# Eight small weight loads in front of the second to fourth K block instead of one per block: a grouped-query attention step on one core

## The chip, the cores and the metric

One NeuronCore of a Trainium2 chip. The metric is the device time of one execution in microseconds (us). A trace's span is 1.8 us shorter than the time of its own execution, so a span must not be compared with a time. A run is called slow when it is over 1.5% above the fastest run of the same kernel in its rounds, and fast otherwise; ratios use fast runs alone.

## The reference

Eight sequences of four query tokens, 32 query heads, 8 key/value heads of 128, a cache of 2048 positions, all bf16.

```python
q = (x @ wq).reshape(B, Sq, Hq, Dh).transpose(0, 2, 1, 3)
k, v = jnp.repeat(k_cache, rep, axis=1), jnp.repeat(v_cache, rep, axis=1)
p = softmax(einsum("bhqd,bhkd->bhqk", q, k) * Dh ** -0.5)
o = einsum("bhqk,bhkd->bhqd", p, v)
out = o.transpose(0, 2, 1, 3).reshape(B, Sq, Hq * Dh) @ wo
```

The caches are 67 MB and have to be read once: 32 blocks of K and 32 of V, 1 MB each (two heads of one sequence, 128 partitions of 8 KB). wq and wo are 4 MB each.

## The kernel before

All loads go out on one queue (the Sync engine's) in one list. The part of wo that is multiplied early is cut so that 480 of its rows lie on 40 partitions; they come in eight small loads of 5 partitions x 12 rows x 1 KB, 60 KB each.

```python
    def load_wo_e(i):
        hi, m = divmod(i, 4)
        rows = wo[: NE * WE, :].rearrange("(q r) j -> q r j", r=WE)      # NE = 40, WE = 12
        a, b = hi * 32 + m, hi * NE // 2 + m
        nc.sync.dma_start(wo_e[a : a + 17 : 4, :, :], rows[b : b + 17 : 4, :, :])
    ...
    load_k(0)
    nc.sync.dma_start(wq_sb[:, :, :], wq.rearrange("(p r) n -> p r n", r=R))
    nc.sync.dma_start(x_sb[:, :], x.flatten_outer_dims())
    loads = []
    for u in range(NU + KA):
        if 1 <= u <= 8:
            loads.append(("e", u - 1))           # one small load in front of each of eight K blocks
        if 0 < u < NU:
            loads.append(("k", u))
        ...
        if u >= KA - 1 and u - KA + 1 < NU:
            loads.append(("v", u - KA + 1))
    ...
    nc.gpsimd.memset(wo_e[:, :, :], 0.0)         # the first small load waits for this, to 5.97 us
```

One thing is not in the code: the framework has eight semaphores for DMAs and hands them out in turn, so each issue waits until the load eight places ahead of it has landed. The Sync queue issues in order, and one that waits holds up all behind it.

The softmax here doesn't subtract the row's maximum and nothing guards it: scores larger than these inputs give would overflow.

## Time and profile before

| | before |
|---|---|
| timed runs, us | 189.18, 189.28, 189.49 |
| the execution that was profiled, us | **192.02** (span 190.2) |
| chain that ended last | 97% DMA |
| DMA, 16 to 51 us / 51 to 170 us | 389 / 424 GB/s |
| TensorE busy | 83% |

How to read it: the chain that ended last is followed back from the last instruction to whatever each step waited for, and 97% of it are loads. So the kernel is one long stream of reads from HBM, and everything else keeps up with it.

### The profile page before, as it was taken

How to read it: one execution, taken by the hardware profiler on the slowest of the kernel's cores; microseconds unless marked ns; L12 is line 12 of the kernel's file. 1: busy time of each engine (PE TensorE's matmuls, PEld its weight loads, DVE VectorE, ACT ScalarE, POOL GpSimd, SP SyncE). 2: the span in 40 equal slices, each digit the busy share in tenths (PEclk: the TensorE clock that was granted, in tenths of full speed). 3: DMA queues.
4: the chain of work that ended last, by engine and by line, in shares of the span. 5: the costliest groups of instructions: out<-in, count | busy, mean ns of one | idle time of the engine just before them, and what ended most of it. 6: DMA issues, size and time to landing. Idle time of an engine off the chain costs nothing.

```text
span 190.2 us, 6461 instructions
## 1 busy us (share of the span) xinstructions
PE 156.9 (83%) x2899; PEld 139.3 (73%) x2899; DVE 113.0 (59%) x218; ACT 86.4 (45%) x170; POOL 6.3 (3%) x9
## 2 busy tenths in 40 slices
PE   0536596999978888999988999978888889999693
PEld 0516396899967777889977888878877778886471
DVE  0580545577756666757766666665666668676420
ACT  2003656565555555445555555554555554454000
POOL 8400000000000000000000000000000000000000
PEclk9999879999999999999999999999999999999858
DMA  6999999999999999999999999999999999999970
GB/s 245 451 407 382 383 394 394 386 385 387 397 419 426 422 426 424 426 422 427 424 424 426 426 422 431 417 427 422 426 424 427 420 429 420 424 424 415 416 310 22
DMA packets 10955, 75.97 MB, mean 399 GB/s; under 512 B 1288, under 2 KB 1416, under 8 KB 2568
## 3 DMA queue, kind: packets, MB, share of 16 engines
q1 hardware_dynamic: 10880, 75.55, 96.4%
q8 instruction: 22, 0.36, 0.7%
q14 instruction: 5, 0.04, 0.1%
q10 hardware_dynamic: 48, 0.02, 0.0%
HBM read 75.53 MB, written 0.03 MB: 397 GB/s over the span
## 4 chain that ended last, share of the span: by engine, by line
DMA 97%; SPq 1%; issue 0%; PE 0%; ACT 0%
DMA k_sb<-in_k_cache_dram 69%; DMA v_sb<-in_v_cache_dram 8%; DMA wo_e<-in_wo_dram 8%; DMA wq_sb<-in_wq_dram 7%; DMA wo_sb<-in_wo_dram 4%; SPq L131 0%; PE out_ps L376 0%; SPq L111 0%; ACT out_sb L430 0%; SPq L121 0%
## 5 line engine op out<-in xcount | busy, mean ns | idle before, releaser
L195 PE MATMUL kp<-ident,k_sb 128*128 128x128 f32 x512 | 82.7, 288 | 20.5 <-DMA k_sb<-in_k_cache_dram 10.5
L202 DVE COPY kt<-kp 128x1024 bf16<-128x1024 bf16 x96 | 65.5, 686 | 28.3 <-PE kp L195 27.4
L266 ACT ACTIVATE probs<-s_ps 64x256 bf16<-64x256 f32 x128 | 48.5, 379 | 69.9 <-PE s_ps L256 69.1
L195 PEld LDWEIGHTS kp<-ident,k_sb 128*128 128x128 f32 x512 | 55.8, 144 | 23.9 <-DMA k_sb<-in_k_cache_dram 12.5
L256 PE MATMUL s_ps<-q_bd,kt 128*128 128x64 bf16 x1024 | 42.5, 195 | 3.1 <-ACT kt L200 1.9
L256 PEld LDWEIGHTS <-kt 128*128 128x128 bf16 x1024 | 40.0, 99 | 5.5 <-ACT kt L200 2.2
L280 PEld LDWEIGHTS <-v_sb 128*128 128x128 bf16 x1024 | 34.4, 96 | 9.5 <-DMA v_sb<-in_v_cache_dram 2.1
L200 ACT COPY kt<-kp 128x1024 bf16<-128x1024 bf16 x32 | 32.4, 1012 | 12.6 <-PE kp L195 11.8
L280 PE MATMUL o_ps<-probs,v_sb 128*128 128x32 bf16 x1024 | 35.1, 177 | 1.2 <-DMA v_sb<-in_v_cache_dram 1.1
L302 DVE TENSOR_REDUCE l_sb<-l_ps 128x32 f32<-128x512 f32 x32 | 22.1, 692 | 21.2 <-PE l_ps L294 21.2
L294 PE MATMUL l_ps<-probs,ones 128*128 128x512 bf16 x64 | 19.0, 379 | 0.0
L306 DVE RECIPROCAL r_sb<-l_sb 128x32 f32<-128x32 f32 x32 | 11.3, 353 | 1.1
L311 DVE TENSOR_TENSOR oT<-o_ps,r_sb 128x32 bf16<-128x32 f32 x32 | 5.8, 182 | 1.9 <-PE o_ps L280 1.7
L294 PEld LDWEIGHTS <-ones 128*128 128x128 bf16 x64 | 6.1, 98 | 0.5
L430 ACT CAST out_sb<-out_ps 64x256 bf16<-64x256 f32 x1 | 0.4, 366 | 13.1 <-PE out_ps L376 13.1
L376 PE MATMUL out_ps<-wo_sb,oP 128*32 128x256 bf16 x48 | 5.5, 393 | 0.1
L171 POOL MEMSET wo_e<- 64x6144 bf16 x1 | 5.2, 5212 | 0.3 <-POOLq L447 0.3
L243 DVE CAST q_bd<-pse 64x512 bf16<-64x512 f32 x4 | 2.6, 683 | 4.3 <-PE pse L234 4.3
L376 PEld LDWEIGHTS <-oP 128*32 128x32 bf16 x48 | 3.5, 137 | 1.4 <-issue 0.2
L178 DVE COPY pick<-ident 128x64 bf16<-128x64 bf16 x4 | 0.6, 220 | 6.5 <-POOL ident masks.py:199 6.5
L219 PE MATMUL psq<-xT_sb,wq_sb 128*128 128x32 bf16 x128 | 3.5, 186 | 0.3 <-DVE xT_sb L213 0.3
L219 PEld LDWEIGHTS <-wq_sb 128*128 128x128 bf16 x128 | 3.5, 103 | 0.3 <-issue 0.3
(41 smaller groups left out, 31.9 us busy)
## 6 DMA issues: line engine op xcount, KB each, us to landing
k_sb<-in_k_cache_dram SPq DMA_DIRECT2D x32, 1024.0 KB, 19.6
v_sb<-in_v_cache_dram SPq DMA_DIRECT2D x32, 1024.0 KB, 19.4
wq_sb<-in_wq_dram SPq DMA_DIRECT2D x1, 4096.0 KB, 14.1
wo_sb<-in_wo_dram SPq DMA_DIRECT2D x4, 512.0 KB, 14.8
wo_sb<-in_wo_dram SPq DMA_DIRECT2D x4, 256.0 KB, 9.6
wo_m<-in_wo_dram SPq DMA_DIRECT2D x1, 512.0 KB
wo_e<-in_wo_dram SPq DMA_DIRECT2D x8, 60.0 KB
x_sb<-in_x_dram SPq DMA_DIRECT2D x1, 32.0 KB
```

The source lines that it names most:

```text
L195: nc.tensor.transpose(kp[:, j, :], k4[:, w : w + 128], ident4[:, :])
L200: nc.scalar.copy(out=kt2, in_=kp2)
L202: nc.vector.tensor_copy(out=kt2, in_=kp2)
L219: nc.tensor.matmul(psq[:, h, :], lhsT=wq_sb[:, r, hh * 128 : (hh + 1) * 128], rhs=xT_sb[:, r, :], start=(r == 0), stop=(r == R - 1),)
L256: nc.tensor.matmul(s_ps[:, 2 * j : 2 * j + 2, :], lhsT=k_t[:, j % (HC // 4), :, e], rhs=q_bd[:, p, e, b, :, :], start=(e == 0), stop=(e == 1),
L266: nc.scalar.activation(out=pr[rows, hf * HC : (hf + 1) * HC, cols], in_=s_ps[rows, :, cols], func=EXP)
L280: nc.tensor.matmul(o_ps[u][:, :], lhsT=vs[u][:, cc, :], rhs=pr[:, cc, :], start=(cc == 0), stop=(cc == C - 1),)
L294: nc.tensor.matmul(l_ps[:, :, :], lhsT=ones[:, :], rhs=pr[:, c : c + LC, :], start=(c == 0), stop=(c + LC == C),)
L302: nc.vector.tensor_reduce(out=l_sb[:, :], in_=l_ps[:, :, :].rearrange("d c q -> d q c"), axis=AX, op=ADD)
L306: nc.vector.reciprocal(r_sb[:, :], l_sb[:, :])
L311: nc.vector.tensor_tensor(out=oT[(p + 1) // 2][:, :, (p == 2) * 1, b, :], in0=o_ps[u][:, :].rearrange("d (h s) -> d h s", h=HP), in1=r_sbs ...
L376: nc.tensor.matmul(out_ps[half * T : (half + 1) * T, :], lhsT=o, rhs=w[:, half * DH : (half + 1) * DH], start=(p == 0 and r == 0), stop=(p ...
```

## The change

The intent is to have the small loads out of the way early: three in front of k1, two in front of k2, three in front of k3, and from then on only blocks of 1 MB.

```diff
     for u in range(NU + KA):
-        if 1 <= u <= 8:
-            loads.append(("e", u - 1))
+        loads += [("e", i) for i in {1: (0, 1, 2), 2: (3, 4), 3: (5, 6, 7)}.get(u, ())]
         if 0 < u < NU:
             loads.append(("k", u))
```

## The prediction

> **What bounds the kernel now.** I read the page's DMA rows first, then the chain that ended last, then one table by stage, then the issues of the DMA queue in order of time, and last the single packets.
>
> ```profile
> span 190.2 us, 6461 instructions
> ...
> PE 156.9 (83%) x2899; PEld 139.3 (73%) x2899; DVE 113.0 (59%) x218; ACT 86.4 (45%) x170; POOL 6.3 (3%) x9
> ...
> DMA  6999999999999999999999999999999999999970
> GB/s 245 451 407 382 383 394 394 386 385 387 397 419 426 422 426 424 426 422 427 424 424 426 426 422 431 417 427 422 426 424 427 420 429 420 424 424 415 416 310 22
> ...
> DMA 97%; SPq 1%; issue 0%; PE 0%; ACT 0%
> DMA k_sb<-in_k_cache_dram 69%; DMA v_sb<-in_v_cache_dram 8%; DMA wo_e<-in_wo_dram 8%; DMA wq_sb<-in_wq_dram 7%; DMA wo_sb<-in_wo_dram 4%; SPq L131 0%; PE out_ps L376 0%; SPq L111 0%; ACT out_sb L430 0%; SPq L121 0%
> ```
>
> The reader should see that the chain is 97% DMA and that the DMA engines are busy from the second slice to the end, so only two things move the time: gaps in the DMA stream, or its speed. There are no gaps to take. But the GB/s row has a step: about 385 in slices 4 to 11, about 424 after. The table by stage (us, busy time of the engines, then clock, DMA share, GB/s) places it:
>
> ```profile
> 16.00:51.00 35.00, 30.83 (x595) 27.85 (x595) 19.54 (x36) 20.42 (x42) 0.00 (x0) 0.95 1.01 389
> 51.00:170.00 119.00, 106.79 (x2042) 96.96 (x2039) 79.50 (x153) 60.79 (x121) 0.00 (x0) 1.00 1.01 424
> ```
>
> The DMA share is 1.01 in both rows, so the engines weren't idle in the slow one; each packet took longer. The trace's packet records say so: a packet of 8 KB took 309 ns before 16 us, 342 ns from 16.1 to 51.1 us, and 309 ns from then on to about 170 us, all engines alike. When one engine was held for 1.1 us by an instruction fetch in the slow stretch, the packets of the others fell to 324 ns. So a shared limit holds there (16 x 8192 B / 342 ns = 383 GB/s), and each engine's own pace later. The loads that this change moves stand in exactly that stretch:
>
> ```profile
> 5.97 0.84 SPq L131 DMA_DIRECT2D wo_e<-in_wo_dram  x1
> ...
> 8.55 0.70 SPq L131 DMA_DIRECT2D wo_e<-in_wo_dram  x1
> 9.29 0.44 SPq L111 DMA_DIRECT2D k_sb<-in_k_cache_dram  x1
> 15.26 0.33 SPq L121 DMA_DIRECT2D v_sb<-in_v_cache_dram  x1
> ...
> 36.29 0.70 SPq L131 DMA_DIRECT2D wo_e<-in_wo_dram  x1
> ```
>
> The first one's packets run at 14.4 to 14.9 us, the last one's at 49.9 to 50.5 us, and its semaphore is complete at 51.16 us: within 0.3 us of the place where packets become fast again. What "wo_e loads in the queue" does to the other engines' packets I can't read from the trace; that the two stretches coincide at both ends I can.
>
> **What the Trainium skill says.** "DMA: Bandwidth & Descriptors", section "Why a DMA increments its semaphore by 16 and not by 1": a load of 5 partitions from the Sync queue is split over 5 DMA engines, the lowest-numbered ones, and the sequencer writes the other 11 counts itself. The trace agrees: the fourth such load (issued at 15.63) has a late group of five counts, at 27.50 to 27.72 us, and from k2 on each 1 MB block completes in two groups, with five counts late (k2: 20.29 to 20.85, and 21.14 to 21.38). Same page, section "Queues, rings and completion order": one engine consumes descriptors in ring order. So these rows cost time on five engines only, and an order changes which packet is early, not how much those five have to move. "HBM Reference", section "Specifications (TRN2)": a core that streams alone gets about 425 GB/s, held by its 16 DMA engines. The fast stretch shows 424; 389 is below that for no reason that the page gives.
>
> **The change, part by part.** No byte, instruction or engine changes, apart from order in the Sync queue: the order of the instructions shows SP alone altered (k1, k2 and k3 now behind 3, 5 and 8 of the small loads). There are eight semaphores for DMAs, used in turn, so an issue waits for the landing of the one eight places ahead of it.
>
> 1. The slow stretch gets shorter (the gain). I follow the five slow engines, ring order x, e0, e1, e2, k1, e3, e4, k2, e5, e6, e7, k3. They finish wq at 14.4 us. Three e packets at about 0.48 us (460 to 507 ns seen) end at 15.9; k1, eight packets at 0.34, at 18.5; e3 and e4 at 19.5; k2 at 22.2; e5 to e7 at 23.7; the last lands some 0.6 us later, at 24.3. The slow stretch would last from 16.1 to about 24 us, 8 us instead of 35. A slow us does 309/342 = 0.904 of a fast one's work, so it loses 0.096 us. Before: 35.0 x 0.096 = 3.4 us. After: 8 x 0.096 = 0.8 us. Gain 2.6 us. All of it is on the path, since the five engines are the last ones and have no gaps to absorb it.
>
> 2. New waits of the queue (no cost expected). k2 is now the tenth issue and waits for wq, complete at 15.24 us; before, it went out at 8.07. The eleven engines without small rows have k1 until 14.4 + 8 x 0.309 = 16.9 us; k2 issued at 15.26 moves some 0.8 us later (the first load: issued 0.73, first packet 1.5), at 16.1. Margin 0.8 us. k3 waits behind three issues of 0.70 us, goes out at about 17.9 and moves at 18.7, while k2 lasts to 19.3 there. v0 waits for k1 on the slow five (landed about 19.2), moves at 20.0, and k3 lasts to about 22. Thin margins, but even where one fails, only those eleven engines idle, which are ahead of the five anyway. The five always have something queued.
>
> 3. Early K blocks land later. On the slow five k1, k2 and k3 land at about 19.2, 22.9 and 27.0 us instead of 18.2, 21.4 and 25.0. TensorE is still at the projection of x then: in order of time its first transpose of k1 starts at 23.88 us, of k2 at about 28 and of k3 at about 31, so each has 4 us of slack. Its later pace, one unit per 4.12 us (norms at 40.08, 44.20, 48.32), is faster than the DMA's 2 x 2.44 = 4.9 us, so a delay would be made up. Cost 0.
>
> 4. Buffers. v6 needs v0's buffer, free at 39.15 us (first write of oT). Its semaphore comes free at about 39.3 in the new order, so the two meet, and the queue then holds seven blocks of 1 MB, 17 us of work. Cost 0.
>
> Sum: 189.28 - 2.6 = 186.7 us if the slow stretch follows the loads.
>
> **The rivals.** (a) The slow stretch belongs to time or to these blocks, not to the small loads (say the way HBM is read while the sixteen engines stand close together in one block). For it: wo_e packets move in only 4.9 of its 35 us, eleven engines never touch wo_e and slow down too, and 15 to 16 us is fast although e0 was then just done. Against it: both ends coincide with the loads. The work of the five is then the same and the time stays at 189.3. (b) The spread between the engines makes it fast: by 51 us the last engines stood over 3 us behind the first. The small loads make that spread, and the change makes it by 24 us rather than 51, so this gives nearly the same gain, about 186.7. (c) The queue starves at 16 to 20 us because k2 waits for wq, with only k1 left in flight: if the margins of part 2 are wrong by 1 us on all engines, +0.5 to +1 us. (d) The whole slow stretch goes, since k1's part of it is the only one left: -3.4 us, and the seven e packets at 460 instead of 507 ns give 0.3 more on the five: 185.6, the most that I can find.
>
> **Range and chances.** I give (step 1 or b) about 0.68, (a) 0.22, (c) without the gain 0.05, (d) 0.05. The centre moves a little from 186.7 towards 189.3: 187.0. The range 185.7 to 189.4 takes in (d) on one side and no effect on the other. Faster by 2% means under 185.5, which is beyond (d): 0.05. Slower by 2% (193.1) has no mechanism that I can see: 0.02. Within 2%: 0.93.
>
> **What would show it right or wrong.** GB/s at 24 to 51 us near 424 instead of 389, 8 KB packets at 309 ns there, and the slow stretch ending when the last wo_e load lands: step 1 right. Still 389 until 51 us: (a). If it turns fast later than 24 us but before 51, (b) is nearer. A DMA share under 0.95 in 16 to 22 us: (c). TensorE idle on k_sb growing by over 2 us and the end moving with it: step 3 wrong. The block k8 landing at about 51.2 us instead of 53.5 to 54.5 would be the gain seen halfway, and the end should move by the same amount.

## The result, and the profile after

| | before | changed |
|---|---|---|
| timed, us | 189.27 median (189.18 to 189.49, 4 runs) | 189.54 median (189.47 to 189.59, 4 runs) |
| ratio | | 1.0012 (95%: 0.9995 to 1.003) |
| profiled execution, us | 192.02 | 189.51 |

A ratio is the mean time of one kernel's fast runs over that of the other's of the same rounds, so it is not quite the ratio of the medians that are quoted.

The page of the changed kernel, the rows of the span and of the GB/s in 40 slices:

```profile
span 187.7 us, 6461 instructions
...
GB/s 204 466 447 356 375 422 424 431 422 424 421 428 415 426 429 419 426 428 426 421 426 426 417 429 428 415 422 433 419 429 426 419 426 426 422 421 418 412 327 34
```

and its table by stage (us; busy time of TensorE, its weight loads, VectorE, ScalarE, GpSimd; clock; DMA share; GB/s):

```profile
16.00:51.00 35.00, 30.86 (x594) 27.88 (x594) 19.48 (x36) 20.39 (x42) 0.00 (x0) 0.95 1.01 414
51.00:170.00 119.00, 110.32 (x2092) 100.42 (x2088) 80.80 (x156) 62.27 (x124) 0.00 (x0) 0.99 1.01 424
```

Read against the profile before, this is the predicted picture: the step in the GB/s row is gone, 8 KB packets (the pieces in which a DMA engine moves a block) take 309 ns from 23 us on, and the span is 2.5 us shorter. Yet the timed runs did not get faster at all. The two profiles are of two executions, and only one of them is like the timed ones: 189.51 against a median of 189.54 for the changed kernel, but 192.02 against 189.28 for the kernel before. So the question became whether the slow stretch (342 ns) belonged to the kernel before at all. A second thing shows in the GB/s row: 356 and 375 in the fourth and fifth slice, where something costs time just after wq. Two single microseconds stand out (the last two columns are DMA share and GB/s):

```profile
17.00:18.00 1.00, 1.00 (x44) 1.00 (x41) 0.00 (x0) 0.39 (x1) 0.00 (x0) 1.00 0.94 270
20.00:21.00 1.00, 0.38 (x1) 0.10 (x1) 1.00 (x2) 0.44 (x2) 0.00 (x0) 1.00 0.94 262
```

The Sync queue's issues there (start us, us, line, load, how many):

```profile
8.27 0.44 SPq L111 DMA_DIRECT2D k_sb<-in_k_cache_dram  x1
8.76 1.41 SPq L131 DMA_DIRECT2D wo_e<-in_wo_dram  x2
15.26 0.34 SPq L111 DMA_DIRECT2D k_sb<-in_k_cache_dram  x1
15.64 2.11 SPq L131 DMA_DIRECT2D wo_e<-in_wo_dram  x3
17.80 0.44 SPq L111 DMA_DIRECT2D k_sb<-in_k_cache_dram  x1
```

and the queue's longest single wait for a load (us in total, times, longest):

```profile
SPq L111 <- DMA wq_sb<-in_wq_dram: 5.1, 1, 5.1
```

The block k2 goes out at 15.26 us, when wq has landed, and k3 at 17.80, behind three small loads.

### The profile page after: what moved, and what is told of

Its sections match the earlier page's. It is cut to its first block, busy times and chain, and to the rows that moved or that the text cites. A ratio compares the mean times of both kernels' runs of the same rounds, so it can differ in the third digit from the quotient of the medians.

```text
span 187.7 us, 6461 instructions
## 1 busy us (share of the span) xinstructions
PE 156.3 (83%) x2899; PEld 139.2 (74%) x2899; DVE 112.5 (60%) x218; ACT 86.4 (46%) x170; POOL 6.3 (3%) x9
## 4 chain that ended last, share of the span: by engine, by line
DMA 97%; SPq 1%; issue 0%; PE 0%; ACT 0%
DMA k_sb<-in_k_cache_dram 73%; DMA v_sb<-in_v_cache_dram 9%; DMA wq_sb<-in_wq_dram 7%; DMA wo_sb<-in_wo_dram 4%; DMA wo_e<-in_wo_dram 4%; SPq L111 0%; SPq L131 0%; PE out_ps L375 0%; ACT out_sb L429 0%; SPq L121 0%
## 5 line engine op out<-in xcount | busy, mean ns | idle before, releaser
L194 PE MATMUL kp<-ident,k_sb 128*128 128x128 f32 x512 | 83.7, 290 | 17.0 <-POOL ident masks.py:199 7.0
L194 PEld LDWEIGHTS kp<-ident,k_sb 128*128 128x128 f32 x512 | 56.6, 146 | 20.0 <-DMA k_sb<-in_k_cache_dram 8.5
L255 PE MATMUL s_ps<-q_bd,kt 128*128 128x64 bf16 x1024 | 43.2, 196 | 3.1 <-ACT kt L199 1.9
L255 PEld LDWEIGHTS <-kt 128*128 128x128 bf16 x1024 | 40.6, 100 | 5.5 <-ACT kt L199 2.2
L375 PE MATMUL out_ps<-wo_sb,oP 128*32 128x256 bf16 x48 | 4.0, 274 | 1.4 <-DMA wo_sb<-in_wo_dram 1.4
L375 PEld LDWEIGHTS <-oP 128*32 128x32 bf16 x48 | 2.4, 95 | 2.5 <-issue 2.4
```

Source lines behind the costliest of these rows:

```text
L194: nc.tensor.transpose(kp[:, j, :], k4[:, w : w + 128], ident4[:, :])
L255: nc.tensor.matmul(s_ps[:, 2 * j : 2 * j + 2, :], lhsT=k_t[:, j % (HC // 4), :, e], rhs=q_bd[:, p, e, b, :, :], start=(e == 0), stop=(e == 1),
L375: nc.tensor.matmul(out_ps[half * T : (half + 1) * T, :], lhsT=o, rhs=w[:, half * DH : (half + 1) * DH], start=(p == 0 and r == 0), stop=(p ...
```

## The experiments

Two theories on the slow stretch. **A**: it is something that single executions fall into, with or without the small loads. **B**: my prediction's, the small loads in the queue cause it. And two on the loss after wq. **S**: a block issued too shortly before the engines need it costs time; and its rival, **T**: small loads standing close together cost time by themselves, on the five engines that move them.

Two readings of the trace's own records recur, and are my arithmetic: the duration of the single 8 KB packets, and the sixteen landings of each block (each DMA engine counts once). The records do not name the engine. In the landings the five engines that move small loads stand apart for the first 50 us as a late group; I call the others "the eleven". Where a diff below shows added lines alone, they stand in place of the two lines that the change removes.

### e1: the kernel before, again

No edit.

> The kernel before, unchanged. The profiled execution of before took 192.02 us, its timed runs 189.28; the profiled execution of the changed kernel took 189.51, its timed runs 189.54. Theory A (the 342 ns stretch was an accident of that one profiled execution): this profile's span is about 187.5 us, 8 KB packets take 309 ns from 16 to 51 us, GB/s there is about 414 to 424. Theory B (my prediction's step 1: small loads in the queue slow all packets): the span is about 190.2 again with 342 ns and 389 GB/s from 16 to 51 us, and the timed runs are then faster for a reason of profiling. Ratio to before 1.000 in both.

Measured: 189.23 us median, ratio 0.999 (0.9976 to 1.0004); profiled execution 189.38 us, span 187.6. One of its six runs took 196.25 (slow). The GB/s row of its page and the rows by stage:

```profile
GB/s 203 468 447 377 425 427 425 422 425 423 431 416 426 425 416 428 430 418 426 432 418 419 437 419 423 421 426 419 425 439 412 426 432 418 423 428 416 404 292 15
...
16.00:51.00 35.00, 31.02 (x570) 28.34 (x574) 19.10 (x35) 19.74 (x40) 0.00 (x0) 0.90 1.01 426
51.00:170.00 119.00, 109.71 (x2086) 101.30 (x2107) 81.10 (x157) 62.86 (x125) 0.00 (x0) 0.99 1.01 424
```

What follows: same kernel, same small loads at the same places (the last one issued at about 35 us), and 426 GB/s where the first profile had 389; no half microsecond from 3 to 167 us has a median 8 KB packet over 309 ns by more than 3. B falls in the form that the prediction gave it, where the loads always bring the stretch. This profile is from here on the "before" to compare with.

### e2, e10, e14: the changed kernel, again

No edit; e2 beside e1, e10 beside e9, e14 beside e13.

> The changed kernel, unchanged, to have five more rounds. Theory A: ratio 1.000 to 1.003, span 187.7, no slow stretch. Theory B: the same time, and a slow stretch of at most 8 us, as in the first profile (none). It also says whether the +0.26 us of the first medians is real.

> The changed kernel once more, in the same rounds as e9. Ratio 1.002 to 1.006. The slow stretch of 342 to 352 ns (seen with small loads in the kernel before, and without any in e7) begins right after wq in the executions that have it; in ten executions of the changed kernel none was over 190.9 us. If the dip after wq breaks it up, none of these will be over 191.5; if not, about one in three will, as for the kernel before.

> The changed kernel beside e13: fast runs in two levels, some at 189.5 and more at 190.3 to 191.0, ratio about 1.004. Executions over 191.5: none in sixteen so far, against eleven in forty-three of the kernel before. If the dip ends the slow stretch, again none or one of six; and e13, which has no dip, should have one or two.

Measured: 190.47, 190.52 and 190.51 us median; ratios 1.005 (1.0028 to 1.0072), 1.005 (1.0012 to 1.0087) and 1.0061 (1.0024 to 1.0098). The eighteen runs lie on two levels: three at 189.55 to 189.62, fifteen at 190.26 to 191.25. All four runs of the first result (189.47 to 189.59) were on the lower level, so that result showed the change too kindly: in the three later series it is about 0.5% slower, still inside 2%. The traces of e2 and e10 are of the upper level, the first one and e14's of the lower. Stretches of e10 and, for comparison, of e1, one us each (columns as before; the last two are DMA share and GB/s). First e10:

```profile
16.00:17.00 1.00, 0.75 (x29) 0.75 (x29) 0.19 (x1) 0.00 (x0) 0.00 (x0) 1.00 0.97 410
17.00:18.00 1.00, 1.00 (x44) 1.00 (x41) 0.00 (x0) 0.39 (x1) 0.00 (x0) 1.00 0.64 197
18.00:19.00 1.00, 1.00 (x45) 1.00 (x42) 0.00 (x0) 0.39 (x1) 0.00 (x0) 1.00 0.62 250
19.00:20.00 1.00, 1.00 (x32) 0.73 (x29) 0.00 (x0) 0.56 (x2) 0.00 (x0) 1.00 0.87 332
20.00:21.00 1.00, 0.39 (x2) 0.10 (x1) 0.95 (x2) 0.44 (x2) 0.00 (x0) 1.00 1.09 360
```

then e1:

```profile
17.00:18.00 1.00, 1.00 (x44) 1.00 (x41) 0.00 (x0) 0.38 (x1) 0.00 (x0) 1.00 1.06 447
18.00:19.00 1.00, 1.00 (x45) 1.00 (x42) 0.00 (x0) 0.43 (x2) 0.00 (x0) 1.00 0.95 401
```

The stream is never interrupted in e1 and has a hole in e10. In the first profile of the changed kernel the hole is shallower (the two rows shown above). Its packet records say what the hole is made of: the eleven are done with k1 at 17.1 us and find k2, issued 1.9 us earlier, but its first packets take 736 to 984 ns on seven of them and 439 to 533 on four, instead of 309. A second set of long packets stands at 20 us, where k3 begins, issued 17.80. So "issued" is not "ready": about 2 us of lead were not enough. A lead of 3.4 us was (v0 in e9: issued 19.17, needed at about 22.6, no long packet). Why some executions fall to 8 to 12 active engines there (e2, e10) and others hardly below 13 (the first profile, e14) I did not settle; in the two bad ones wq landed 0.1 us later (15.37 and 15.36 against 15.24 and 15.29 us).

### e3: the small loads late

```diff
-        if 1 <= u <= 8:
-            loads.append(("e", u - 1))
+        if 9 <= u <= 16:
+            loads.append(("e", u - 9))
```

> The eight small loads still one per K block, but in front of the tenth to the seventeenth K block instead of the second to the ninth. Theory A: same time as before within 0.3 us, ratio 0.998 to 1.001, no slow stretch anywhere. Theory B: a slow stretch of some 35 us moves to about 55 to 100 us, span about 190. If the place of the loads is really neutral (they cost the five engines the same 8 x 0.46 us wherever they stand), ratio 1.000.

Measured: 189.20 us, ratio 0.999 (0.9974 to 1.0006), no slow stretch in its profile, one run of 196.16. Here the place of the small loads is neutral; no block comes late. Moving them moved no slow stretch, but the profiled run was a fast one, so by itself that says little.

### e4, e6: all eight in front of k1; three and five

```diff
+        if u == 1:                                  # e4
+            loads += [("e", i) for i in range(8)]
+        loads += [("e", i) for i in {1: (0, 1, 2), 2: (3, 4, 5, 6, 7)}.get(u, ())]     # e6
```

> All eight small loads in front of the second K block. The eight semaphores make k1 wait until the first small load has landed, after wq, at about 15.5 us; it is issued about 16.7 and moves about 17.5, so the DMA engines have a real gap after wq (about 3 us on the eleven, under 1 us on the five that move small loads meanwhile). Theory A with the five engines as the bound: +0.3 to +1.2 us (ratio 1.002 to 1.006). Theory B: the slow stretch ends before 20 us and the time is 2 us shorter in profile.

> Three small loads before the second K block and five before the third: k2 now waits for wq and for five issues of 0.70 us, so it goes out at about 17.4 to 18.2 us. Theory S: a dip of about 2.5 us on the eleven engines instead of 1.1; those engines end about 1.2 us ahead of the five (last landing 182.9 against 184.1), so the time rises by about 2.4 - 1.2 = 1.2 us, ratio 1.005 to 1.010, between the changed kernel and the one with all eight in front (1.015). Rival T: as e5.

Measured: e4 192.30 us, ratio 1.0154 (1.0135 to 1.0174; the verdict at 2% is "unclear"); e6 190.95 us, ratio 1.0081 (1.0067 to 1.0096). e6 came as expected; e4 lost more than twice the upper end of its expectation. In e4:

```profile
16.00:17.00 1.00, 0.82 (x31) 0.82 (x31) 0.13 (x1) 0.00 (x0) 0.00 (x0) 1.00 0.29 123
17.00:18.00 1.00, 1.00 (x45) 1.00 (x42) 0.00 (x0) 0.39 (x1) 0.00 (x0) 1.00 0.59 147
18.00:19.00 1.00, 1.00 (x44) 1.00 (x41) 0.00 (x0) 0.44 (x2) 0.00 (x0) 1.00 0.66 225
```

A share of 0.29 is about the five engines alone (5/16 = 0.31). The landings suggest why idle time of the eleven, which I had called free, is paid for (first and last of the sixteen, us):

```
                     k1             k2             k8             last load of wo
e1 (before)      17.40  18.25   19.83  21.12   46.81  50.87   178.77  184.09
changed, first   17.55  19.05   20.41  22.69   47.95  52.06   179.54  184.27
e10 (changed)    17.52  19.25   20.78  22.98   48.35  52.22   179.91  185.21
e6               17.48  19.10   22.71  24.45   49.70  52.34   181.28  185.92
e4               21.15  22.19   23.60  25.51   50.70  52.59   182.93  187.41
```

In e1 the last load ends on two engines at 183.97 and 184.09, and on the other fourteen by 182.90. The small loads put the five some 3.7 us behind, but by the end most of the others are behind too (I put it down to the 22 instruction fetches, 0.9 to 1.1 us each in the first profile, which hold one engine at a time; not tested), and only 184.09 - 182.90 = 1.2 us are left between them. My reading is that a hole on the eleven is free up to about 1.2 us and costs its full length beyond. By the first landing of k2 against e1 the holes are 0.6 us (changed, first profile), 1.0 (e10), 2.9 (e6) and 3.8 (e4). 2.9 - 1.2 = 1.7 and 3.8 - 1.2 = 2.6; the last landings are 1.8 and 3.3 us later. So the reading fits e6. In e4 0.7 us is left over, and there the five lost time themselves: the packets of the seventh small load, issued 15.35, took 511 to 1255 ns instead of 460. In e10 the last landing is 1.1 us later, though a hole of 1.0 should be free; there the first landing hides that half of the eleven landed k2 at about 22.3 us, over 2 us late.

### e5: k2 in front of the wait

```diff
+        loads += [("e", i) for i in {1: (0, 1, 2), 3: (3, 4, 5, 6, 7)}.get(u, ())]
```

> Three small loads in front of the second K block, none before the third, five before the fourth: k2 no longer waits for wq. Theory S (the changed kernel is slower only because k2 goes out after wq, so that the DMA engines run dry at 17 to 18.5 us): no dip of active DMA engines there, k1 to k3 land on the eleven engines as in the kernel before (17.4, 20.0, 22.5 us), ratio 0.999 to 1.001. Rival T (many small loads close together cost time by themselves, on the five engines): ratio 1.003 to 1.006 as in the changed kernel, or more.

Measured: 190.43 us, ratio 1.0061 (1.0029 to 1.0093), runs from 189.53 to 191.51. A miss (theory S had 0.999 to 1.001), and an unclean experiment: the hole at 17 us is gone, but k3 now waits behind five small loads until 18.05 and its first packets are long (20 to 21 us), and the profiled execution had a slow stretch of its own, 342 ns from 16 to 20 us. It does not tell S from T.

### e7: no small loads

```diff
-        if 1 <= u <= 8:
-            loads.append(("e", u - 1))
```

> The eight small loads are left out (wrong result on purpose: those rows of wo stay zero). If the five engines set the end alone and by all of their extra work: -3.7 us. If, as the landings of the kernel before show, the other eleven end only about 1.2 us earlier: -1.0 to -1.3 us, ratio 0.993 to 0.995. If slow executions (over 191 us) still come among its runs, they have nothing to do with the small loads.

Measured: runs of 188.26, 188.29, 188.33, 188.34, 190.47 and 191.32 us, ratio 0.9966 (0.9926 to 1.0007); the result is wrong. The four quickest are 0.9 us under the 189.2 of e1 (190.47 still counts as fast, hence the wide interval): the five engines' 3.7 us of extra work is worth only about 0.9, near the 1.2 of the landings. The profile fell in a slow execution (191.32 us):

```profile
GB/s 235 436 436 363 377 377 375 379 382 424 422 422 424 420 425 424 429 420 429 422 425 420 432 415 436 413 429 422 425 422 431 420 425 427 418 423 418 412 265 32
```

There it is again, 375 to 382 GB/s from the fifth slice to the ninth, with not one small load in the program: packets of 352 ns from 15.5 to 42 us. B is dead, and A's half "without the small loads" is shown.

### e8: heavier small loads

```diff
-    wo_e = const.tile([64, WE, D], BF16, name="wo_e")
+    wo_e = const.tile([64, 2 * WE - 1, D], BF16, name="wo_e")
-        rows = wo[: NE * WE, :].rearrange("(q r) j -> q r j", r=WE)
+        rows = wo[: NE * (2 * WE - 1), :].rearrange("(q r) j -> q r j", r=2 * WE - 1)
...
-    nc.gpsimd.memset(wo_e[:, :, :], 0.0)
+    nc.gpsimd.memset(wo_e[:, :WE, :], 0.0)
```

> Each small load carries 23 rows per partition instead of 12 (wrong result on purpose), at the same places: 8 x 11 KB = 90 KB more for each of five engines, 3.4 us at 26.5 GB/s. If the five engines set the end: +3.2 to +3.6 us, ratio 1.017 to 1.019. If they have slack: less. The 8 KB packets of the other eleven stay at 309 ns whatever the small loads weigh; Theory B would have them at 342 ns.

Measured: 192.64, 195.12, 195.35, 195.63, 197.97, 198.5 us, ratio 1.0264 (1.0204 to 1.0324). Its output is wrong, which doesn't matter for the time. The profiled run is the fastest, +3.4 us over e1's 189.2, as expected when the five set the end: its last load lands on eleven engines by 183.02 us and on five at 185.72 to 187.39. (The 26.5 GB/s of the expectation are 8192 B in 309 ns.) From 2.5 to 170 us no half microsecond of its trace has a median 8 KB packet over 309 ns. Why its other five runs were so much longer no trace shows (two of them still count as fast, hence the ratio), and they are not used.

### e9 and e11: x in front of wq

```diff
     load_k(0)
-    nc.sync.dma_start(wq_sb[:, :, :], wq.rearrange("(p r) n -> p r n", r=R))
     nc.sync.dma_start(x_sb[:, :], x.flatten_outer_dims())
+    nc.sync.dma_start(wq_sb[:, :, :], wq.rearrange("(p r) n -> p r n", r=R))
```

e9 is the changed kernel with this edit, e11 the kernel before with it.

> The changed kernel with the loads of x and wq exchanged, nothing else: k2, the tenth issue, then waits for x (landed by about 7 us) and no longer for wq (15.24). Theory S (the loss comes from k2 going out after wq): no dip at 17 to 18.5 us, k2 lands on the eleven engines at about 19.9 instead of 20.5; a small dip of at most 0.5 us is left before k3, which still waits behind three issues of 0.70 us. Ratio 0.999 to 1.002 and below the changed kernel of the same rounds. Rival T (the small loads close together cost by themselves): same ratio as the changed kernel.

> The control of e9: the kernel before with x in front of wq. Its queue never ran dry, so nothing is to be gained: ratio 0.999 to 1.001, some slow executions of 192 to 196 us among its runs as among those of before.

Measured: e9 189.93 us, ratio 1.0016 (0.9978 to 1.0054), against 190.52 for the changed kernel of the same rounds (e10); one of its six runs took 192.48 (slow). The tenth issue now waits for x, so k2 goes out at 10.19 us:

```profile
8.75 1.40 SPq L131 DMA_DIRECT2D wo_e<-in_wo_dram  x2
10.19 0.44 SPq L111 DMA_DIRECT2D k_sb<-in_k_cache_dram  x1
15.38 2.11 SPq L131 DMA_DIRECT2D wo_e<-in_wo_dram  x3
17.54 0.44 SPq L111 DMA_DIRECT2D k_sb<-in_k_cache_dram  x1
```

On the eleven k2 lands at 19.85 to 20.20 us, as in e1 (19.83 to 20.18), and the hole at 17 us is closed. The one before k3 is left (k3 issued 17.54, needed at 19.5, first packets up to 1233 ns). So for k2 the hole closes when the block is issued earlier, as S says; the interval is too wide to read the gain from. e11: 189.70 us, ratio 0.999 (0.9941 to 1.0038), three of seven runs at 193.5 to 194.2. Its profile is one of these, with long packets already from 6 us on, during wq (1359 ns for its 32 KB packets where e1 has 1213, that is 340 per 8 KB), and until 52 us; a slow stretch need not begin after wq.

### e12: the kernel before, a third time

> The kernel before again, in the same rounds, for the share of slow executions and, if the profile falls in one, for the stretch in which its packets take longer: it should begin at 15 to 16 us, right after wq, and end where an engine is held by an instruction fetch, at a different place than 51 us, which no wo_e load marks.

Measured: 189.47 us, ratio 1.0013 (0.9962 to 1.0063), runs of 191.58 (still counted as fast) and 193.44 among the six. The profile fell in a fast run (189.16 us) and shows no slow stretch and 425 GB/s from 16 to 51 us, as e1.

### e13: small loads close together, no block late

```diff
+        loads += [("e", i) for i in {1: (0, 1, 2), 2: (3,), 4: (4, 5, 6, 7)}.get(u, ())]
```

together with x in front of wq.

> All eight small loads are still issued within the first 20 us (three before k1, one before k2, four before k4), with x in front of wq, but k1, k2 and k3 all go out before wq lands, so each block is in the queue 3 us or more before the engines need it. Theory S (only a block issued too late costs): 16 engines active at 415 to 430 GB/s from 15 to 26 us, k1, k2, k3 and v0 on the eleven engines at 17.4, 20.0, 22.5 and 25.0 us, end as before, ratio 0.999 to 1.001. Rival T (small loads close together cost by themselves): ratio 1.002 to 1.006.

Measured: 189.29 us median, ratio 0.9989 (0.995 to 1.0028; wide, since a run of 191.45 of the kernel before still counts as fast); five runs at 189.15 to 189.50, two at 192.83 and 193.46, beside 190.51 for the changed kernel in the same rounds. Three and four small loads stand together (three, two and three in the changed kernel), but k1, k2 and k3 go out before wq lands:

```profile
8.27 0.44 SPq L111 DMA_DIRECT2D k_sb<-in_k_cache_dram  x1
8.76 0.71 SPq L131 DMA_DIRECT2D wo_e<-in_wo_dram  x1
9.51 0.91 SPq L111 DMA_DIRECT2D k_sb<-in_k_cache_dram  x2
16.58 0.33 SPq L121 DMA_DIRECT2D v_sb<-in_v_cache_dram  x1
16.95 4.30 SPq L131 DMA_DIRECT2D wo_e<-in_wo_dram  x4
```

The last small load goes out at 20.60 us (17.10 in the changed kernel), so they are not quite as early. The five fast runs are those of the kernel before and do not overlap with the changed kernel's (189.58 to 191.25). T falls in the size that it was given; S is left, and e4 and e6, where a block goes out later still and more is lost, go the same way. Its profile again fell in a slow execution, 340 to 342 ns per 8 KB from 6 to 51.5 us, although its last small load had landed by 31.2 us: a third trace against B.

### Does the change end the slow stretch?

e14's trace begins like the slow ones. Its 8 KB packets take 340 to 342 ns from 16.0 to about 17.4 us. Then k2's long first packets come, and from about 17.4 us on all others take 309 ns again. In e5 the slow stretch ended at 20 us in just that way, at k3's long packets. In the first profile of the kernel before it ended between 50.9 and 51.3 us, beside an instruction load (50.87 us) and one packet of 968 ns (51.22). The stretches of e7, e11 and e13 ended in the same way, within half a microsecond of the start of an instruction load (41.71, 52.02 and 51.67 us); but earlier loads of this kind passed in each of these traces without ending it, so what ends a stretch is open. Over all timed executions told here (the profiled one of 192.02 us is left out), the kernel before (the runs that e1 to e14 were timed against, the first four, e1 and e12) took more than 191.3 us in 11 of 44, with none between 189.82 and 191.45, and the changed kernel in 0 of 22, the highest being 191.25 (at one in four, 22 in a row by chance would be 0.75^22 = 0.2%). The means of all executions, slow ones included, are 190.27 and 190.28 us: if the hole does end the stretch, what it costs in most executions is about what it saves in a quarter of them. This is a count, not a proof: only four of the 22 were traced, the limit before e14 ran was 191.5 (with it, 10 of 44 and 0 of 22), the executions were on more than one chip, and what starts the stretch is not known. In the traces it began at 6 or at 15.5 to 16 us; whether something outside the kernel starts it, on the same HBM or elsewhere, was not tested.

## Why the prediction was wrong

The predicted time was 187.0 us, the range ended at 189.4, the result was 189.54.

1. **"The slow stretch gets shorter (the gain)", 2.6 us.** This is the step that failed. The reasoning went from a coincidence in one trace (the small loads and the slow packets stood in the same 35 us) to a cause. e1 has the loads without the stretch, e7 the stretch without the loads, e13 the stretch for 20 us after the loads. Nothing was there to be won: a typical execution of the kernel before has 309 ns from the start. What spoke against it stood in the numbers I had: 192.02 us for the profiled execution, 189.28 for the timed ones. The 2.74 us between them are four fifths of the 3.4 us that I took for the stretch's cost.
2. **"New waits of the queue (no cost expected)".** The wait was found (k2 waits for wq, issued at 15.26) and two of its terms were mis-sized. The first: "moves some 0.8 us later", taken from the start of the first load's packets. That start was misread: the records put it at 1.73 us, not 1.5, so 1.0 us after the issue. And the start is not the whole: the trace before already showed that those first packets take up to 1284 ns; here k2's took up to 984 ns, and the one that began first was done 2.9 us after the issue (17.13 + 0.98 - 15.26). The second: the eleven "are ahead of the five anyway" by the small loads' 3.7 us. At the end it is 1.2 us (e1's landings), 0.9 by e7's fast runs. Rival (c), which I gave 0.05 without the gain, is what happened: +0.3 us at first, about +1 in e2, e10 and e14. The sign that I had named for it, a DMA share under 0.95 from 16 to 22 us, was not there in the first profile (0.98 over the six us) and was in e10 (0.85). The range had no room for it: 189.3 and 0.5 to 1 us more lie above its end.
3. **"Early K blocks land later", cost 0.** Right. k1, k2 and k3 were to land at 19.2, 22.9 and 27.0 us on the five and did at 19.05, 22.69 and 26.51. The last chain stayed 97% DMA.
4. **"Buffers", cost 0.** Right: the queue's waits for TensorE are 0.5 and 0.4 us in the whole changed trace.
5. **The rivals.** (a), "the slow stretch belongs to time or to these blocks", had the nearest time, 189.3, but by luck: it kept the stretch, and its sign (389 GB/s until 51 us) did not come; (b), a spread between the engines, stays possible as a reason why a stretch ends, but it too forecast nearly the same gain, which did not come, because a typical execution has no stretch.
6. **The signs.** I had named GB/s near 424 after 24 us, packets of 309 ns and k8 at about 51 us as proof of step 1. All came (424 GB/s, 309 ns, k8 at 51.0 to 51.1 us on four of the five and 52.06 on the last), and step 1 was still wrong. Signs that compare two single executions can't test a cause that differs from execution to execution.
7. **A small misreading.** "With five counts late" holds for k2 in the trace before; k3 and v0 have six late counts there (24.28 to 25.04 us for k3), since another engine had fallen behind by then. Nothing rests on it.

## What to carry to other kernels

Before reasoning from a profile, set the profiled execution's own time beside the timed ones; where they differ by as much as the effect one hopes for, profile the unchanged kernel once more. In this stream, which is limited by DMA, the small loads cost little by their bytes (0.9 us for all eight), but each takes one of the eight places in flight, and a large block behind it may go out too late: a lead of about 2 us left a hole and 3.4 us did not. Before calling idle time on engines that "have slack" free, read from the landings of the last load how much slack is left at the end: here 1.2 us of 3.7.

## What the Trainium skill lacked or had wrong

- "DMA: Bandwidth & Descriptors", section "Latency and other measured facts", gives about 600 ns to the first byte for loads issued from the Sync queue. The trace does not contradict it: the first load's packets start 1.0 us after its issue instruction begins and 0.63 us after it ends (0.73 + 0.37 us, first packet at 1.73). But these packets last up to 1284 ns instead of 309, and a block issued 1.9 us before it was needed (k2 of the changed kernel) still began with packets of up to 984 ns, done 2.9 us after the issue. The page has no figure for the lead that a block needs in such a stream; about 2 us left a hole, 3.4 us did not.
- "HBM Reference", section "Specifications (TRN2)", has about 425 GB/s for a core that streams alone. The trace agrees for most of the time (424), but some executions stay at 375 to 390 GB/s for 1 to 46 us of their first 52, with the packets of all sixteen engines 10% to 14% longer (340 to 352 ns instead of 309). No page describes such a state of a core's lone stream.
- "Perfetto Trace Analysis" does not say to check that the profiled execution is a typical one; here it was 192.02 us against 189.28.
- On the choice of engines ("DMA: Bandwidth & Descriptors", section "Why a DMA increments its semaphore by 16 and not by 1") there is nothing to mend, the traces agree: 5 late counts for each small load, and five late landings of sixteen for the first blocks behind them (k1 and k2 of the changed kernel; further on other engines fall behind as well).
